# Attention of a fused chain in pairs of tiles: outputs of two tiles in one block, scores of the next two in another

## The chip, the cores and the metric

One Trainium2 chip, one NeuronCore. The metric is device microseconds of one execution. Its engines are TensorE (PE, with its weight loads shown as PEld), VectorE (DVE), ScalarE (ACT), GpSimd (POOL) and SyncE (SP, which only issues DMAs here). Each runs its own instructions in the order of the program and waits on semaphores.

## The reference

Three layers after each other, in float32. The first is a linear attention with decay over (4 batches, 8 heads, 768 steps, head size 48):

```
for t in range(S):
    cur = einsum('bhd,bhe->bhde', u * k[t], v[t])
    y[t] = einsum('bhd,bhde->bhe', r[t], state + cur)
    state = w * state + einsum('bhd,bhe->bhde', k[t], v[t])
```

Its output, as 3072 tokens of 384, goes through an expert with three first matrices, `h = max(x @ w1, x @ w2, x @ w3)` (384 to 768) and `h @ w_out`, and then through a normalised gated one, `silu(xn @ w_gate) * (xn @ w_val) @ w_out` (384 to 1536 to 384).

## The kernel before

**Attention in tiles.** The 768 steps are cut into 6 chunks of 128; with 4 batches that makes 24 tiles, tile i being chunk i // 4 of batch i % 4. Within a tile the recurrence is done as matmuls:

- `prep` (L266): VectorE multiplies the raw r and k of the tile by powers of the decay (L264, the "raw product"); POOL makes r * u * k (L272, L273).
- `prep_b` (L276): VectorE reduces that over each head (L280), and POOL puts the sums on the diagonals of the eight 128 x 128 matrices Dg (L283). `prep2` (L288): POOL scales k for the products (L291).
- `pe_a` (L293): the **scores**, 8 matmuls of 48 x 128 by 128 columns, two beside each other in the two row halves of the array, into two PSUM banks. The profile shows each float32 matmul of attention as two records. `mix` (L303): VectorE copies the scores under the causal mask into Dg, two instructions, one per bank.
- `pe_y` (L336): the **outputs**, matmuls of 128 x 32 by 128 columns in four column strips, from Dg and v and, from tile 4 on, from the state. The longest strip has nine after each other. `fin` (L361): ScalarE writes the rounded output into x (L370), VectorE the rest (L371).
- `pe_st` (L315): the **products** of k and v, 8 matmuls of 128 x 64 by 48 columns. ScalarE masks them into kv (L313, two instructions; kv has one buffer), POOL decays the state (L332) and adds kv (L334). For tiles 0 to 3 the mask writes the state itself; the last four tiles have no products.

**The expert in slots.** The first expert goes in six rounds u, one for each chunk of 128 steps and 4 batches, 512 columns. A round has 18 slots of the first matrices (`a_l1`, L399) and 6 of the second (`a_out`, L426); each has nine 128 x 128 matmuls (three products of rounded and residual parts, L71 to L73) of 512 columns into one of four PSUM banks, which ScalarE copies (L417) or VectorE takes the maximum of (L420). In round 0 the first six and the next six slots have 256 columns, so that there are 30.

**What sets the order.** The order on each engine is that of the program. The list `steps` holds three steps per tile; six are done before round 0. After each slot a number of further steps is done: in round 0 one after each of slots 0 to 3 and the rest spread over slots 6 to 24; in rounds 1 to 4 twelve steps over the first 20 of 24 slots, after slots 0, 1, 3, 5, 6, 8, 10, 11, 13, 15, 16 and 18. So round u does the tiles of round u + 1. `block(i)` is scores and mix of tile i + 1, then outputs, x and products of tile i, and puts the loads of tile i + 3 into the list `loads`, from which `load_next` takes. Raw inputs have three buffers, Dg two. Scores, outputs and products take turns in four PSUM banks (`psx`).

**The weights.** `tick` (L163) converts one piece of the weights from 64-bit words: a load on SP (L96) whose buffer comes free with the piece's sign step, three conversions on ScalarE (L107 to L109), two steps on VectorE (L118, L122), and for the first expert a cast on ScalarE (L129) and a residual on POOL or VectorE (L130). Round 0 has a tick after nearly every slot, rounds 1 to 4 nine each, of which three end with sums of weights on VectorE (L137). After attention come the last round and the second expert, which the change does not touch.

The state of the pair's two tiles belongs to different batches, so neither tile waits for the other's state.

Of the kernel before, what the change touches and what calls it, by code (L numbers as in the profile page):

```python
# [9 lines left out]
F32 = mybir.dt.float32  # L10
# [8 lines left out]
B, H, S, D = 4, 8, 768, 48  # L19
# [14 lines left out]
NB = S // 128  # L34
NT = B * NB
NP = H // 2
# [3 lines left out]
def r32(ap):  # L40
    return ap.bitcast(F32)
# [3 lines left out]
def rwkv_moe_kernel(ctx, tc, rkT, rkv, wd, ub, cst, rg, w1p, wo1p, w2p, out):  # L45
# [6 lines left out]
    psx = ctx.enter_context(tc.tile_pool(name="psx", bufs=4, space=PSUM))  # L52
# [138 lines left out]
    def load_next(n=1):  # L191
        for _ in range(n):
            if loads:
                loads.pop(0)()

    def load_tile(i):
        if i >= NT:
            return
        a = tp.tile([128, 2, NP, 128], F32, tag="raw", bufs=3, name=f"raw{i}")
        t = tp.tile([128, VO + NP * 144], F32, tag="tm", bufs=3, name=f"tm{i}")  # L200
        raw_t[i], tm_t[i] = a, t
        loads.append(lambda: sync.dma_start(a[0:64], rows64[96 * i:96 * i + 64]))
        if i < NT - 1:
            loads.append(lambda: sync.dma_start(a[64:128], rows64[96 * i + 48:96 * i + 112]))
        else:
            loads.append(lambda: (sync.dma_start(a[64:112], rows64[96 * i + 48:96 * i + 96]),
                                  sync.dma_start(a[112:128], rows64[96 * i:96 * i + 16])))
        loads.append(lambda: sync.dma_start(t[:, 0:VO], rkv[i, :, 0:VO]))
        loads.append(lambda: sync.dma_start(t[:, VO:], rkv[i, :, VO:]))
# [45 lines left out]
    st = {}  # L255

    def prep_raw(i):
        raw = raw_t.pop(i)
        st[i] = dict(raw=raw, tm=tm_t.pop(i))
        if i == 0:  # L260
            dve.tensor_tensor(out=raw[:, 1], in0=raw[:, 1], in1=qk[:, 1], op=ALU.mult)
            dve.tensor_tensor(out=raw[:, 0], in0=raw[:, 0], in1=qk[:, 0], op=ALU.mult)
        else:
            dve.tensor_tensor(out=raw, in0=raw, in1=qk, op=ALU.mult)  # L264

    def prep(i):  # L266
        prep_raw(i)
        s = st[i]
        tm = s["tm"]
        ru = tp.tile([128, DM], F32, tag="ru", name=f"ru{i}")  # L270
        eng = dve if i < NRU else pool
        eng.tensor_tensor(out=ru, in0=tm[:, 0:DM], in1=usb, op=ALU.mult)  # L272
        eng.tensor_tensor(out=ru, in0=ru, in1=tm[:, DM:2 * DM], op=ALU.mult)  # L273
        s["ru"] = ru

    def prep_b(i):  # L276
        s = st[i]
        a8 = tp.tile([128, H], F32, tag="a8", bufs=2, name=f"a8{i}")
        ru = s["ru"]
        dve.tensor_reduce(out=a8, in_=ru.rearrange("p (h d) -> p h d", d=D), op=ALU.add,  # L280
                          axis=mybir.AxisListType.X)
        Dg = tp.tile([128, H, 128], F32, tag="Dg", bufs=2, name=f"Dg{i}")
        pool.affine_select(out=Dg, in_=a8.unsqueeze(2).to_broadcast([128, H, 128]),  # L283
                           pattern=[[0, H], [1, 128]], channel_multiplier=-1, base=0,
                           compare_op=ALU.is_equal, fill=0.0)
        s["Dg"] = Dg

    def prep2(i):  # L288
        if i // B < NB - 1:
            k = st[i]["tm"][:, DM:2 * DM]  # L290
            pool.tensor_tensor(out=k, in0=k, in1=kt, op=ALU.mult)  # L291

    def pe_a(i):  # L293
        s = st[i]
        raw = s["raw"]
        pa = [psx.tile([128, NP, 128], F32, tag="x", name=f"pa{i}_{j}") for j in range(2)]
        for pr in range(NP):
            for j in range(2):
                sl = slice(64 * j, 64 * j + 48)
                pe.matmul(pa[j][:, pr], raw[sl, 1, pr], raw[sl, 0, pr], start=True, stop=True)  # L300
        s["pa"] = pa

    def mix(i):  # L303
        s = st[i]
        dg = s["Dg"].rearrange("p (r j) t -> p r j t", j=2)
        for j in range(2):
            dve.copy_predicated(out=dg[:, :, j], mask=cmask.unsqueeze(1).to_broadcast([128, NP, 128]),  # L307
                                data=s["pa"][j])

    def mask_kv(o, pk):  # L310
        for j in range(2):
            sl = slice(48 * j, 48 * j + 48)
            act.activation(o[:, :, sl], pk, AF.Copy, scale=m01[j])  # L313

    def pe_st(i):  # L315
        s = st[i]
        c, b = divmod(i, B)
        if c == NB - 1:
            return
        tm = s["tm"]  # L320
        v3 = tm[:, VO:].rearrange("p (r q e) -> p r q e", q=3, e=D)
        pk = psx.tile([128, NP, D], F32, tag="x", name=f"pkv{i}")
        for pr in range(NP):
            for j in range(2):
                o = DM + 96 * pr + 48 * j
                pe.matmul(pk[64 * j:64 * j + 64, pr], tm[:, o:o + 64], v3[:, pr, 2 * j], start=True, stop=True)
        if c == 0:
            mask_kv(Tst[b], pk)
        else:
            kv = tp.tile([128, NP, 96], F32, tag="kv", name=f"kv{i}")  # L330
            mask_kv(kv, pk)
            pool.tensor_tensor(out=Tst[b], in0=Tst[b],  # L332
                               in1=w128.unsqueeze(2).to_broadcast([128, NP, 96]), op=ALU.mult)
            pool.tensor_tensor(out=Tst[b], in0=Tst[b], in1=kv, op=ALU.add)  # L334

    def pe_y(i):  # L336
        s = st[i]
        c, b = divmod(i, B)
        tm = s["tm"]
        py = s["py"] = psx.tile([128, 3, 128], F32, tag="x", name=f"py{i}")  # L340
        lanes = []
        for n in range(4):
            lane = []
            for k in range(3):
                pr, o = (k, 32 * n) if n < 3 else (3, 32 * k)
                ops = [(tm[:, VO + 144 * pr + 48 * j + o:VO + 144 * pr + 48 * j + o + 32],
                        s["Dg"][:, 2 * pr + j]) for j in range(2) if o != (64, 0)[j]]
                if c > 0:
                    ops.append((Tst[b][:, pr, o:o + 32], s["raw"][:, 0, pr]))
                for m, (l, r) in enumerate(ops):  # L350
                    lane.append((py[32 * n:32 * n + 32, k], l, r, m == 0, m == len(ops) - 1))
            lanes.append(lane)
        for m in range(max(map(len, lanes))):
            for lane in lanes:
                if m < len(lane):
                    o, l, r, start, stop = lane[m]
                    pe.matmul(o, l, r, start=start, stop=stop)  # L357
# [3 lines left out]
    def fin(i):  # L361
        s = st[i]
        u, m = divmod(i, B)
        if m == 0:
            xt[u] = ap_.tile([128, 2, 3, 512], F32R, tag="x", bufs=2, name=f"x{u}")
        xh, xl = xt[u][:, 0], xt[u][:, 1]
        o = 128 * m
        cs = slice(o, o + 128)
        y = s["py"]
        act.copy(xh[:, :, cs], y)  # L370
        dve.tensor_tensor(out=xl[:, :, cs], in0=y, in1=r32(xh[:, :, cs]), op=ALU.subtract)  # L371

    def att_steps():
        def block(i):
            if i + 1 < NT:
                pe_a(i + 1)
                mix(i + 1)
            pe_y(i)
            fin(i)
            pe_st(i)  # L380
            load_tile(i + 3)

        def ahead(i):
            load_next(2)
            prep(i)

        def ahead_b(i):
            load_next(1)
            prep_b(i)
            prep2(i)  # L390

        for i in range(NT):
            yield lambda i=i: block(i)
            yield lambda i=i: ahead(i + 2) if i + 2 < NT else None
            yield lambda i=i: ahead_b(i + 2) if i + 2 < NT else None

    hs, sB = {}, {}

# [44 lines left out]
    with tc.manual_schedule():  # L443
# [14 lines left out]
        for _ in range(WARM):  # L458
            pe.matmul(pw[:, 0:128], r32(ones), r32(ones), start=True, stop=True)
        steps = list(att_steps())  # L460
        pos = 0
        tick(TKI[0])
# [578 lines left out]
```

## Time and profile before

| | |
|---|---|
| median of 3 runs | 868.15 us (867.7 to 873.35) |
| the profiled execution | 869.46 us |
| its span, first to last instruction | 867.4 us |
| mean granted TensorE clock | 0.973 of 2.4 GHz |
| instructions | 13472 |

The span is that of the profiled execution alone; the 2.06 us beside it lie before the first and after the last instruction. In the rows below, times are us from the span's start, mean durations ns; a name such as `pl<-x,w_a` says which tile an instruction writes and from which it reads (pl a slot's bank, pa scores, py outputs, pkv products).

### The profile page before, as it was taken

The page shows a single profiled execution, that of the slowest core. Times are in us where ns is not written, and L with a number is a line of the kernel's source. Part 1 is how long each engine was busy: PE and PEld are TensorE (multiplying, and loading weights), DVE is VectorE, ACT ScalarE, POOL GpSimd, SP SyncE. Part 2 cuts the span into 40 slices and gives each one's busy share as a digit, 9 for nine tenths or more (in the row PEclk, how much of TensorE's full clock was granted, in tenths as well). Part 3 has the DMA queues.
Part 4 walks back from the last instruction along what each step waited for, and adds up shares of the span by engine and source line. Part 5 has one row for each costly group of instructions (what it writes and reads, how often), then busy time and mean ns, then how long its engine had stood idle before and what let it go on. Part 6 is the DMA issues. An engine that isn't in the chain of part 4 may idle for free.

```text
span 867.4 us, 13472 instructions
## 1 busy us (share of the span) xinstructions
PE 835.2 (96%) x5206; PEld 688.8 (79%) x5206; DVE 496.6 (57%) x752; ACT 406.3 (47%) x762; POOL 253.5 (29%) x215
## 2 busy tenths in 40 slices
PE   7779899999999999999989999999999999999996
PEld 6667788888888888887778788888788888888885
DVE  5779957857858757525745464644445372333342
ACT  1776643434434433315367564555544454444441
POOL 3589645435435432005547442000100000000000
PEclk7689999999999999999989999999999999999998
DMA  9675646666665665153376551345251062433001
GB/s 260 211 229 161 197 142 176 183 186 173 187 186 173 185 187 151 58 181 132 113 281 235 194 208 56 118 174 187 105 189 56 0 255 91 142 131 110 1 36 40
DMA packets 48915, 131.87 MB, mean 152 GB/s; under 512 B 6982, under 2 KB 19782, under 8 KB 44236
## 3 DMA queue, kind: packets, MB, share of 16 engines
q1 hardware_dynamic: 46684, 115.01, 41.6%
q0 software_dynamic: 1728, 14.16, 4.1%
q10 hardware_dynamic: 432, 1.77, 0.6%
q8 instruction: 43, 0.70, 0.3%
q14 instruction: 28, 0.23, 0.1%
HBM read 97.08 MB, written 33.84 MB: 151 GB/s over the span
## 4 chain that ended last, share of the span: by engine, by line
PE 85%; DVE 6%; ACT 2%; DMA 2%; POOL 2%; issue 2%; SPq 0%; DVEq 0%; ACTq 0%; POOLq 0%
PE pl L71 7%; PE pl L73 7%; PE pl L72 7%; PE py L357 5%; PE po L71 5%; PE po L73 5%; PE po L72 5%; PE px L72 4%; PE px L71 4%; PE px L73 4%; PE pb L71 3%; PE pb L73 3%; PE pa L71 3%; PE pa L73 3%; PE pb L72 3%; PE pa L72 3%
## 5 line engine op out<-in xcount | busy, mean ns | idle before, releaser
L71 PE MATMUL pl<-x,w_a 128*128 128x512 f32 (+1 forms) x342 | 133.4, 390 | 5.9 <-ACT w_a L129 2.8
L73 PE MATMUL pl<-x,w_a 128*128 128x512 f32 (+1 forms) x342 | 130.7, 382 | 0.7 <-POOL w_a L130 0.7
L72 PE MATMUL pl<-x,w_a 128*128 128x512 f32 (+1 forms) x342 | 130.5, 382 | 0.2 <-DVE x L371 0.2
L815 DVE TENSOR_TENSOR v<-pb,es 128x512 f32<-128x512 f32 x36 | 24.9, 692 | 165.7 <-PE pb L73 165.7
L71 PEld LDWEIGHTS pl<-x,w_a 128*128 128x128 f32 x342 | 65.2, 191 | 19.7 <-ACT w_a L129 3.0
L420 DVE TENSOR_TENSOR c<-pl,c 128x512 f32<-128x512 f32 (+1 forms) x76 | 50.0, 658 | 49.2 <-PE pl L73 43.7
L73 PEld LDWEIGHTS pl<-x,w_a 128*128 128x128 f32 x342 | 65.4, 191 | 13.5 <-POOL w_a L130 1.1
L72 PEld LDWEIGHTS pl<-x,w_a 128*128 128x128 f32 x342 | 65.4, 191 | 11.7 <-DVE x L371 0.4
L724 ACT CAST hb<-si 128x512 fp32r<-128x512 f32 x36 | 22.3, 620 | 80.6 <-DVE si L818 80.6
L122 DVE TENSOR_TENSOR wf<-wraw 128x384 f32<-128x384 f32 x60 | 59.9, 999 | 0.0
L422 ACT CAST h1h<-c 128x512 fp32r<-128x512 f32 (+1 forms) x32 | 19.0, 593 | 75.3 <-DVE c L420 75.0
L541 POOL TENSOR_TENSOR sq<-sq 128x512 f32<-128x512 f32 x12 | 16.3, 1361 | 123.9 <-ACT sq L539 79.5
L283 POOL TENSOR_SCALAR_AFFINE_SELECT Dg<-a 128x1024 f32<-128x1024 f32 x24 | 31.1, 1295 | 72.2 <-DVE a L280 58.3
L357 PE MATMUL py<-Dg,tm 128*32 128x128 f32 x768 | 51.1, 304 | 0.0
L118 DVE SCALAR_TENSOR_TENSOR wraw<-wf,wraw 128x384 uint32<-128x384 uint32 x60 | 50.1, 836 | 0.1
L504 POOL TENSOR_TENSOR ws<-gv,ws 128x576 fp32r<-128x576 f32 x24 | 36.9, 1537 | 42.3 <-ACT ws L503 37.0
L307 DVE COPY_PREDICATED Dg<-csb,pa 128x512 f32<-128x512 uint32 x48 | 32.7, 735 | 27.1 <-PE pa L300 23.9
L357 PEld LDWEIGHTS py<-Dg,tm 128*32 128x32 f32 x768 | 42.6, 121 | 4.6 <-issue 1.4
L71 PE MATMUL pb<-f,ws 128*128 128x512 f32 x108 | 42.6, 395 | 0.3 <-ACT pb L793 0.3
L72 PE MATMUL pa<-f,ws 128*128 128x512 f32 x108 | 42.5, 394 | 0.0
L71 PE MATMUL pa<-f,ws 128*128 128x512 f32 x108 | 42.5, 394 | 0.0
L73 PE MATMUL pa<-f,ws 128*128 128x512 f32 x108 | 42.5, 394 | 0.0
(176 smaller groups left out, 2131.3 us busy)
## 6 DMA issues: line engine op xcount, KB each, us to landing
ws<-w2s SPq DMA_DIRECT2D x24, 1152.0 KB, 5.1
wraw<-in_w2p SPq DMA_DIRECT2D x36, 384.0 KB, 3.5
w2s<-ws POOLq DMA_DIRECT2D x12, 1152.0 KB, 6.0
raw<-in_rkT SPq DMA_DIRECT2D x47, 256.0 KB, 4.2
tm<-in_rkv SPq DMA_DIRECT2D x24, 384.0 KB, 4.9
tm<-in_rkv SPq DMA_DIRECT2D x24, 288.0 KB, 4.9
wraw<-in_w1p SPq DMA_DIRECT2D x18, 384.0 KB, 4.0
w2d<-wf SPq DMA_DIRECT2D x36, 192.0 KB, 3.7
```

Of the source, the lines that this page charges most:

```text
L71: pe.matmul(o, lh, rh, start=start, stop=False, **kw)
L72: pe.matmul(o, lh, rl, start=False, stop=False, **kw)
L73: pe.matmul(o, ll, rh, start=False, stop=stop, **kw)
L118: dve.scalar_tensor_tensor(out=clow(n), in0=cw[n].bitcast(U32), scalar=3, in1=clow(n), op0=ALU.logical_shift_left, op1=ALU.bitwise_or)
L122: dve.tensor_tensor(out=cw[n], in0=clow(n).bitcast(F32), in1=csgn(n), op=ALU.mult)
L283: pool.affine_select(out=Dg, in_=a8.unsqueeze(2).to_broadcast([128, H, 128]), pattern=[[0, H], [1, 128]], channel_multiplier=-1, base=0, c ...
L307: dve.copy_predicated(out=dg[:, :, j], mask=cmask.unsqueeze(1).to_broadcast([128, NP, 128]), data=s["pa"][j])
L357: pe.matmul(o, l, r, start=start, stop=stop)
L420: dve.tensor_tensor(out=c1[:, :n], in0=p[:, :n], in1=c1[:, :n], op=ALU.max)
L504: lo_eng.tensor_tensor(out=t[:, 1, sl], in0=r[:, sl], in1=r32(t[:, 0, sl]), op=ALU.subtract)
L724: act.copy(hh, x)
L815: dve.tensor_tensor(out=v1, in0=Bk, in1=es, op=ALU.add)
```

## The change

Tiles 0 to 3 keep their order, without the scores of tile 4 in the block of tile 3. From tile 4 on the steps go in pairs. One step does the outputs of tiles i and i + 1, their x, then the products of both into one PSUM bank, the state updates and the list entries of the loads of tiles i + 3 and i + 4. Four steps prepare the tiles i + 2 and i + 3. A sixth does the scores of both, into all four banks of `psx`, and both mixes. The number of steps stays 72, so the spreading over slots is the same: in round 0 scores(4,5) come after slot 7 and outputs(4,5) after slot 8, scores(6,7) after slot 16 and outputs(6,7) after slot 17; in rounds 1 to 4 outputs come after slots 0 and 10, scores after slots 8 and 18. No arithmetic is changed.

```diff
-    def pe_st(i):
+    def pe_st(i, pk=None):
...
-        pk = psx.tile([128, NP, D], F32, tag="x", name=f"pkv{i}")
+        if pk is None:
+            pk = psx.tile([128, NP, D], F32, tag="x", name=f"pkv{i}")
...
+        s["pk"] = pk
+
+    def state(i):
+        c, b = divmod(i, B)
+        if c == NB - 1:
+            return
+        pk = st[i]["pk"]
...
-        def block(i):
-            if i + 1 < NT:
-                pe_a(i + 1)
-                mix(i + 1)
-            pe_y(i)
-            fin(i)
-            pe_st(i)
-            load_tile(i + 3)
+        def scores(*tiles):
+            for i in tiles:
+                pe_a(i)
+            for i in tiles:
+                mix(i)
+
+        def outputs(*tiles):
+            for i in tiles:
+                pe_y(i)
+            for i in tiles:
+                fin(i)
+            pk = None
+            if len(tiles) > 1 and tiles[0] // B < NB - 1:
+                pk = psx.tile([128, 2, NP, D], F32, tag="x", name=f"pkv{tiles[0]}")
+            for n, i in enumerate(tiles):
+                pe_st(i, pk if pk is None else pk[:, n])
+            for i in tiles:
+                state(i)
+                load_tile(i + 3)
...
-        for i in range(NT):
-            yield lambda i=i: block(i)
-            yield lambda i=i: ahead(i + 2) if i + 2 < NT else None
-            yield lambda i=i: ahead_b(i + 2) if i + 2 < NT else None
+        for i in range(3):
+            yield lambda i=i: (scores(i + 1), outputs(i))
+            yield lambda i=i: ahead(i + 2)
+            yield lambda i=i: ahead_b(i + 2)
+        yield lambda: outputs(3)
+        yield lambda: ahead(5)
+        yield lambda: (ahead_b(5), scores(4, 5))
+        for i in range(4, NT, 2):
+            yield lambda i=i: (outputs(i, i + 1), load_next(2))
+            for j in (i + 2, i + 3):
+                yield lambda j=j: ahead(j)
+                yield lambda j=j: ahead_b(j)
+            yield lambda i=i: scores(i + 2, i + 3) if i + 2 < NT else None
```

## Rows read from the trace of the kernel before

**Rows 1.** The page, busy us (share of the span) and instructions of each engine.

```profile
PE 835.2 (96%) x5206; PEld 688.8 (79%) x5206; DVE 496.6 (57%) x752; ACT 406.3 (47%) x762; POOL 253.5 (29%) x215
```

**Rows 2.** Windows: stretch, its length, busy us (count) by engine, clock, DMA share, GB/s.

```profile
64.00:89.40 25.40, 20.91 (x188) 17.16 (x187) 23.97 (x29) 16.75 (x37) 22.85 (x20) 1.00 0.61 178
...
125.70:361.80 236.10, 236.10 (x2060) 195.38 (x2059) 167.46 (x250) 97.29 (x191) 93.18 (x76) 1.00 0.58 168
...
59.80:63.20 3.40, 3.40 (x55) 3.03 (x55) 1.53 (x2) 2.59 (x6) 3.32 (x4) 0.50 0.97 275
```

**Rows 3.** TensorE's waits, 31.8 to 107 us: total us, times, longest.

```profile
PE pa L300 <- issue: 5.2, 2, 3.3
```

**Rows 4.** Timeline of TensorE around tile 17's block: start, length, records; windows cut some.

```profile
270.05 0.39 PE L73 MATMUL pl<-x,w_a 128*128 128x512 f32 x1
...
270.37 1.05 PE L300 MATMUL pa<-raw 48*128 48x128 f32 x14
...
270.37 1.16 PE L300 MATMUL pa<-raw 48*128 48x128 f32 x16
...
273.24 0.38 PE L357 MATMUL py<-raw,T 128*32 128x128 f32 x2
...
273.55 0.56 PE L326 MATMUL pkv<-tm 128*64 128x48 f32 x12
...
273.55 0.67 PE L326 MATMUL pkv<-tm 128*64 128x48 f32 x16
...
274.49 0.39 PE L72 MATMUL pl<-x,w_a 128*128 128x512 f32 x1
```

**Rows 5.** The same around tile 22's block (no products) and tile 23's (outputs alone).

```profile
348.14 0.39 PE L73 MATMUL pl<-x,w_a 128*128 128x512 f32 x1
...
351.98 0.40 PE L72 MATMUL pl<-x,w_a 128*128 128x512 f32 x1
...
361.79 0.39 PE L73 MATMUL pl<-x,w_a 128*128 128x512 f32 x1
...
364.53 0.39 PE L72 MATMUL pl<-x,w_a 128*128 128x512 f32 x1
```

**Rows 6.** Timeline of VectorE in round 0; in brackets its idle time before.

```profile
63.67 0.55 DVE L280 TENSOR_REDUCE a<-ru 128x8 f32<-128x384 f32 x1 [2.34 <-POOL ru L273]
...
71.92 1.53 DVE L264 TENSOR_TENSOR raw<-raw,qk 128x1024 f32<-128x1024 f32 x1
...
94.78 1.38 DVE L307 COPY_PREDICATED Dg<-csb,pa 128x512 f32<-128x512 uint32 x2
```

**Rows 7.** Timeline of POOL in round 0.

```profile
64.55 1.42 POOL L283 TENSOR_SCALAR_AFFINE_SELECT Dg<-a 128x1024 f32<-128x1024 f32 x1
...
69.10 1.22 POOL L334 TENSOR_TENSOR T<-T,kv 128x384 f32<-128x384 f32 x1
```

**Rows 8.** Timeline of ScalarE in round 0.

```profile
67.50 0.42 ACT L313 ACTIVATE kv<-pkv,csb 128x192 f32<-128x192 f32 x1
...
71.18 0.37 ACT L417 COPY c<-pl 128x256 f32<-128x256 f32 x1
71.45 0.56 ACT L107 ACTIVATE wf<-wraw 128x384 f32<-128x384 f32 x1
```

**Rows 9.** Timeline of TensorE in round 0: two scores blocks, slots 9 and 18.

```profile
59.35 1.91 PE L300 MATMUL pa<-raw 48*128 48x128 f32 x16 [1.96 <-issue]
...
64.83 0.39 PE L71 MATMUL pl<-x,w_a 128*128 128x256 f32 x1
...
89.40 1.30 PE L300 MATMUL pa<-raw 48*128 48x128 f32 x16 [3.29 <-issue]
...
94.89 0.50 PE L71 MATMUL pl<-x,w_a 128*128 128x512 f32 x1
```

**Rows 10.** Timeline of VectorE in rounds 1 and 2.

```profile
187.16 0.29 DVE L137 TENSOR_TENSOR wf<-wf,wf 128x128 f32<-128x128 f32 x1 [2.43 <-DMA w2d<-wf]
...
215.97 1.48 DVE L420 TENSOR_TENSOR c<-pl,c 128x512 f32<-128x512 f32 x2
```

More of the change, by code (lines that the diff above doesn't have):

```diff
@@ L373, in att_steps @@
     def att_steps():
-        def block(i):
-            if i + 1 < NT:
-                pe_a(i + 1)
-                mix(i + 1)
-            pe_y(i)
-            fin(i)
-            pe_st(i)
-            load_tile(i + 3)
+        def scores(*tiles):
[16 more added lines that the diff above has]
+                load_tile(i + 3)
         def ahead(i):
-            load_next(2)
-            prep(i)
+            if i < NT:
+                load_next(2)
+                prep(i)
         def ahead_b(i):
-            load_next(1)
-            prep_b(i)
-            prep2(i)
-        for i in range(NT):
-            yield lambda i=i: block(i)
-            yield lambda i=i: ahead(i + 2) if i + 2 < NT else None
-            yield lambda i=i: ahead_b(i + 2) if i + 2 < NT else None
+            if i < NT:
+                load_next(1)
+                prep_b(i)
+                prep2(i)
+        for i in range(3):
[11 more added lines that the diff above has]
+            yield lambda i=i: scores(i + 2, i + 3) if i + 2 < NT else None
     hs, sB = {}, {}
```

## The prediction, made before the changed kernel was run

> **What bounds the kernel now.** I read the busy shares first: TensorE is busy 96% of the span, VectorE 57% [rows 1]. A share mixes stages, so the table of windows comes next [rows 2]. From 125.7 to 361.8 us, where attention is spread between the expert's slots, TensorE is busy 236.10 of 236.10 us at full clock: there every microsecond of TensorE work saved is saved from the end. From 64.0 to 89.4 us VectorE is busy 23.97 of 25.40 us, POOL 22.85, TensorE 20.91: that stage is paced by the weight conversion together with attention's VectorE and POOL steps. The table of waits says so too: between 31.8 and 107 us TensorE stands 5.2 us before two scores blocks [rows 3]. So the change must be costed twice: as TensorE work in rounds 1 to 4, as order on VectorE, ScalarE and POOL in round 0.
>
> **What the switches cost.** Slot matmuls start 0.227 us apart. Around one attention block the last slot matmul starts at 270.05 and the second one after it at 274.49 [rows 4]; less two pitches that is 3.99 us. Its contents: scores, 8 pairs at 0.11 (14 records span 1.05 us, 16 span 1.16), 0.88; outputs, 18 steps of the longest column strip (9 matmuls, two records each) at 0.11, the step by which two records outlast one of 0.27 [rows 4], 1.98; products, 8 pairs at 0.055 (12 records 0.56, 16 records 0.67), 0.44 [rows 4]. Together 3.30, so four changes of kind (slot, scores, outputs, products, slot) cost 0.69. The block without products is 351.98 - 348.14 - 0.45 = 3.39, of it 0.53 for three changes; the block of tile 23, outputs alone, is 364.53 - 361.79 - 0.45 = 2.29, of it 0.31 for two [rows 5].
>
> A pair of tiles has eight changes now, 1.38 us. Then it has five. The outputs block: 0.31 plus 0.16 for the products, 0.47. The scores block between two slots is not in the trace. It costs at least 0.22 (what scores add to an outputs block) and at most 0.53 (the three changes of the block without products); I take 0.42, nearest to the other two-change block, a little above it because the first scores pair starts late in its block too. The second tile of a block adds only contents. Saved per pair: 1.38 - 0.47 - 0.42 = 0.49 us.
>
> Rounds 1 to 4, tiles 8 to 23: before 12 x 0.69 + 3 x 0.53 + 0.31 = 10.2; after 6 x 0.47 + 2 x 0.31 + 7 x 0.42 = 6.4. **Gain 3.8 us** (2.9 to 5.2 by the two bounds). All of it lies on the path, TensorE being without a pause there. In round 0 the same count gives 5 x 0.69 - 0.47 - 2 x 0.47 - 3 x 0.42 = 0.8 us, but that stage has pauses to lose it in; it is inside the next sum.
>
> **Round 0, the order.** Now mix(4) runs five slots ahead of its outputs. Then scores(4,5) come after slot 7, in VectorE's order behind the reduce of tile 5, and outputs(4,5) after slot 8. The reduce waits for POOL and ends at 63.67 + 0.55 = 64.22 [rows 6]; nothing ahead of it changes but mix(4), and VectorE's wait for POOL hides that removal. A tile's mix takes 1.38 us for its two halves [rows 6], so mix(4) ends at about 65.6; mix(5) needs the diagonal that POOL ends at 64.55 + 1.42 = 65.97 [rows 7] and ends at 67.4. Scores(5) start at 59.35 now, behind their raw product [rows 9], and still do; with slot 8 behind them TensorE is through before 63. **The added wait**: it stands some 3 us until 65.6. Behind it: outputs 2 x 1.98, products 2 x 0.44, changes 0.4, slot 9 at about 71.0, against 64.83 [rows 9]. Of these 6.2 us, 2.4 are tile 5's own work done early.
>
> Who waits for that: SP's load of tile 7 (raw 4's buffer; needed 15 us later, free), POOL's decay of the state, and ScalarE. There the buffer kv is single: the masked products of tile 5 must wait until POOL has added those of tile 4 (1.22 us [rows 7]). Chain: products end 70.9, masks 2 x 0.42, add 1.22, masks 2 x 0.42, then what is queued on ScalarE: four conversions and casts of some 0.56, and the copy of slot 9's bank, 0.37 [rows 8], which ends at about 76.4 instead of 71.55. VectorE's maximum and the raw product of tile 6 stand behind that copy, so the product shifts from 71.92 [rows 6] to about 76.7: **VectorE is 4.8 us late**. It was nearly always busy from here to mix(7), which ended at 94.78 + 1.38 = 96.16 [rows 6]; part of its wait for the copy and the low half of tile 5, done early, come back, so I take 98.5 (96.2 if all is caught up, 101.0 if nothing). Outputs(6,7) wait for it after slot 17: outputs(6) from 97.1, outputs(7), products, slot 18 at about 102.2 against 94.89 [rows 9]. Less 2.4 us for tile 7's work done early, 4.9 us. A pause of this length lowers the clock: after the 1.96 us pause before 59.35 [rows 9] the granted clock was 0.50 from 59.8 to 63.2 [rows 2], 1.2 GHz for 3.4 us, worth up to 1.7 us. I add half of that beyond what the pause of 3.29 us before 89.40 [rows 9] brings already: **loss about 5.7 us**. Bounds: if VectorE catches up fully, the pause before 89.40 goes too and the stage gains 1.2; if nothing is caught up and two more stretches run at half clock, it loses 10.
>
> **Sum.** +5.7 - 3.8 = +1.9. The profiled execution took 869.46 us (span 867.4, 2.1 around it), 1.3 above the median of 868.15; it would become 871.4, and the median 870.0. All later phases keep their instructions.
>
> **The rivals.**
> *Absorbed (0.27).* Round 0 is paced by VectorE's and POOL's total, which does not change; the late scores wait where TensorE now waits anyway. For it: 4.5 of 25.4 us of TensorE idle in the window from 64.0 to 89.4 [rows 2]. Against it: the reduce at 63.67 is now directly ahead of the mix that outputs wait for. 868.15 - 1.2 - 3.8 = 863.
>
> *Slower (0.10): VectorE late in every round.* In rounds 1 to 4 scores come after slot 8 and their outputs after slot 10, 2 x 2.04 us later. From the end of slot 8 TensorE has the scores block, 2 x 0.88 + 0.42, and two slots before it asks for the first mix, 6.3 us; a mix takes 1.38, so the rival decides once VectorE is over 4.9 us behind at slot 8. For it: the weight sums of slot 6's conversion lie just ahead; in round 2 VectorE did two maxima in a row at 215.97 [rows 10], so it was about a slot, 2 us, behind, and another such sum waited 2.43 us for a DMA [rows 10], together 4.4. A wait of 1.5 us and half a stretch of low clock, 1.7, in four rounds: 870 + 12.8 = 883. Against it, all four rounds must come out so.
> The Trainium skill (TensorEngine Tiling (Array Packing), PSUM Bottleneck) says that tiling makes TensorE faster but not the emptying of PSUM, which can become the limit. The rows have the prices: TensorE fills the four banks in 1.76 us and VectorE empties them in 2 x 1.38 = 2.76; by that rule this rival holds wherever one or two slots lie between.
>
> *The change saves no switch (0.08).* If the second tile of a block started as late as a new kind does, rounds 1 to 4 would stay as they are and only round 0's loss count: 868.15 + 5.7 = 874. Against it: within a kind no step of rows 4 is late.
>
> **How the numbers follow.** The forecast has 0.55. Its own range is 864 to 876, from the bounds above. With the absorbed case the range is 863 to 877, which leaves out its lower half and nearly all of the slower rival, under 2 in 10. This kernel's measurement can tell about 1% from no change, 8.7 us: faster needs the absorbed case with the upper gain and more, 0.03; slower is most of the slower rival, 0.08; the same 0.89.
>
> **What would show it.** In the changed profile: blocks of the pair in rounds 1 to 4 with one change into and one out of each, TensorE still without pauses from 126 us, and attention's last block some 3.8 us earlier relative to slot 0 of round 1. In round 0: a pause before outputs(4) ended by VectorE's mix, ScalarE waiting for POOL's add between two masks, a longer pause before outputs(6). Wrong: no wait before either outputs block, or waits for the mix in rounds 1 to 4, or a scores block whose two changes cost over 0.53 us.

## The result, and the profile after

The changed kernel takes 877.58 us (median of 4 runs, 874.82 to 879.19) beside 868.35 us for the kernel before on the same chip: ratio 1.0096, 95% interval 1.0068 to 1.0123. It is **slower by 9.2 us**, about 1%. I had forecast +1.9 us, a median of 870.0 and a range up to 877.0, so the direction was right, the size was too small by 7 us, and the median lies 0.6 us above the range (by the ratio, 868.15 x 1.0096 = 876.5, just inside it). The profiled execution took 879.19 us, its span is 877.4 (before 867.4) and its mean granted clock 0.964 (before 0.973).

The page of the changed kernel first: busy us, share of the span and instructions of each engine.

```profile
PE 838.7 (96%) x5206; PEld 692.4 (79%) x5206; DVE 497.2 (57%) x752; ACT 407.2 (46%) x762; POOL 254.9 (29%) x215
```

Beside [rows 1] no engine has more instructions, and TensorE is 3.5 us busier with the same 5206. It should have been less busy, by the switches saved. Some of its work must have run slower, so I looked for the clock. These are the windows of the changed kernel (columns as in rows 2), the two pair blocks of outputs in round 0 first, then the stretch behind a wait in round 1, then one block in round 1 that had no wait, then most of rounds 1 to 4.

```profile
64.70:71.60 6.90, 6.86 (x112) 5.85 (x112) 3.71 (x7) 1.30 (x3) 3.48 (x4) 0.57 0.40 116
98.90:105.90 7.00, 7.00 (x113) 5.86 (x113) 3.80 (x7) 2.35 (x5) 2.09 (x3) 0.58 0.55 163
162.90:166.30 3.40, 3.40 (x10) 2.72 (x9) 3.29 (x8) 1.59 (x3) 0.00 (x0) 0.51 0.02 7
137.00:141.00 4.00, 4.00 (x113) 3.86 (x112) 0.56 (x1) 1.07 (x2) 0.83 (x1) 1.00 0.18 48
170.00:374.20 204.20, 204.20 (x1792) 171.09 (x1785) 143.55 (x215) 85.32 (x167) 78.62 (x64) 1.00 0.58 169
```

The same 112 or 113 matmul records of a pair's outputs take 4.0 us at clock 1.00 in round 1 and 6.9 to 7.0 us at 0.57 and 0.58 in round 0: most of each block ran at 1.2 GHz. In 170.0 to 374.2 us TensorE has no gap and full clock, as before in 125.7 to 361.8 [rows 2].

What stood ahead of the slow stretches is in the changed kernel's table of TensorE's waits, first from 31.8 to 107 us (total, times, longest):

```profile
PE py L365 <- issue: 3.9, 1, 3.9
...
PE py L365 <- POOL w_a L130: 2.1, 1, 2.1
...
PE pa L300 <- ACT w_a L129: 1.5, 1, 1.5
```

and then the longest from 107 to 374.2 us:

```profile
PE psok L248 <- DVE Dg L307: 1.9, 1, 1.9
```

Of the two waits before scores of [rows 3] the longer is gone, and of the other 1.5 us are left (pa). In addition TensorE now waits before both outputs blocks (py), 2.1 and 3.9 us. The row of the 2.1 us names POOL; but the outputs read Dg, and VectorE's mix of tile 4 starts at 63.92 and takes 1.33 us for its two halves (below), so its first half ends just before the outputs start at 64.74. I had not foreseen the wait in the second table at all.

Where the time went, from the changed kernel's timeline of TensorE (start, length, records, in brackets the idle time before). The starts of slots 9 and 18 and of slot 0 of round 1 serve as marks.

```profile
64.74 0.43 PE L365 MATMUL py<-Dg,tm 128*32 128x128 f32 x2 [2.11 <-POOL w_a L130]
...
72.83 0.39 PE L71 MATMUL pl<-x,w_a 128*128 128x256 f32 x1
...
98.89 0.43 PE L365 MATMUL py<-Dg,tm 128*32 128x128 f32 x2 [3.94 <-issue]
...
106.97 0.50 PE L71 MATMUL pl<-x,w_a 128*128 128x512 f32 x1
...
134.89 0.39 PE L71 MATMUL pl<-x,w_a 128*128 128x512 f32 x1
...
162.69 0.19 PE L248 MATMUL psok<-ok,csb 128*1 128x4 f32 x2 [1.94 <-DVE Dg L307]
```

Slot 0 of round 1 in the kernel before:

```profile
123.59 0.39 PE L71 MATMUL pl<-x,w_a 128*128 128x512 f32 x1
```

Against [rows 9], slot 9 is 72.83 - 64.83 = 8.0 us later and slot 18 is 106.97 - 94.89 = 12.1; less the 2.4 us for the tile done early that is 9.7 of loss where I had 4.9 and 0.8 for the clock, 5.7. Slot 0 of round 1 is 134.89 - 123.59 = 11.3 later, 0.88 of it the scores of tile 9, done already: **round 0 loses 10.4**. The wait of psok (the decay flag) is 1.94, and 3.40 us at half clock behind it lose 1.7; the distance between the same slots of the two kernels grows there by 3.4. Rounds 1 to 4 give back 3.6 by their blocks (worked out below). 10.4 + 3.4 - 3.6 = 10.2, beside a difference of the spans of 10.0.

How the lateness came about on the other engines, VectorE first (changed kernel, round 0):

```profile
63.45 0.55 DVE L280 TENSOR_REDUCE a<-ru 128x8 f32<-128x384 f32 x1 [2.34 <-POOL ru L273]
63.92 1.33 DVE L307 COPY_PREDICATED Dg<-csb,pa 128x512 f32<-128x512 uint32 x2
...
77.89 0.43 DVE L450 TENSOR_TENSOR c<-pl,c 128x256 f32<-128x256 f32 x1 [4.02 <-ACT c L447]
78.23 1.53 DVE L264 TENSOR_TENSOR raw<-raw,qk 128x1024 f32<-128x1024 f32 x1
...
98.06 2.57 DVE L307 COPY_PREDICATED Dg<-csb,pa 128x512 f32<-128x512 uint32 x4
```

and ScalarE:

```profile
71.87 0.48 ACT L378 CAST x<-py 128x384 fp32r<-128x384 f32 x1 [2.40 <-PE py L365]
...
73.27 0.41 ACT L313 ACTIVATE kv<-pkv,m 128x192 f32<-128x192 f32 x1
...
74.87 0.42 ACT L313 ACTIVATE kv<-pkv,csb 128x192 f32<-128x192 f32 x1 [1.19 <-POOL T L342]
...
77.50 0.36 ACT L447 COPY c<-pl 128x256 f32<-128x256 f32 x1
```

This is the predicted chain, link for link: reduce, mix, outputs, ScalarE's cast, its 1.19 us for POOL's add between two masks because kv has one buffer, its copy of slot 9's bank, then VectorE's maximum (which stood 4.02 us for that copy) and the raw product of tile 6 behind it. But the product starts at 78.23 where I had 76.7, and mix(7) ends at 100.6 where I had 98.5. The excess starts in the outputs block: 2.9 us of slow clock there.

### The profile page after: what moved, and what is told of

The parts are those of the page before. It is cut to its first block, busy times and chain, and to the rows that moved or that the text cites. A ratio compares the mean times of both kernels' runs of the same rounds, so it can differ in the third digit from the quotient of the medians.

```text
span 877.4 us, 13442 instructions
## 1 busy us (share of the span) xinstructions
PE 838.7 (96%) x5206; PEld 692.4 (79%) x5206; DVE 497.2 (57%) x752; ACT 407.2 (46%) x762; POOL 254.9 (29%) x215
## 4 chain that ended last, share of the span: by engine, by line
PE 79%; DVE 7%; POOL 6%; ACT 3%; DMA 2%; issue 2%; SPq 0%; DVEq 0%; POOLq 0%; ACTq 0%
PE pl L71 6%; PE py L365 6%; PE pl L72 6%; PE pl L73 6%; PE po L73 5%; PE po L71 5%; PE po L72 5%; PE px L72 4%; PE px L71 4%; PE px L73 4%; PE pb L71 3%; PE pb L73 3%; PE pa L71 3%; PE pa L73 3%; PE pb L72 3%; PE pa L72 3%
## 5 line engine op out<-in xcount | busy, mean ns | idle before, releaser
L71 PE MATMUL pl<-x,w_a 128*128 128x512 f32 (+1 forms) x342 | 134.6, 394 | 6.7 <-ACT w_a L129 2.8
L73 PE MATMUL pl<-x,w_a 128*128 128x512 f32 (+1 forms) x342 | 132.4, 387 | 2.9 <-POOL w_a L130 2.9
L72 PE MATMUL pl<-x,w_a 128*128 128x512 f32 (+1 forms) x342 | 132.3, 387 | 0.0
L71 PEld LDWEIGHTS pl<-x,w_a 128*128 128x128 f32 x342 | 66.3, 194 | 21.1 <-ACT w_a L129 3.0
L73 PEld LDWEIGHTS pl<-x,w_a 128*128 128x128 f32 x342 | 66.6, 195 | 16.3 <-POOL w_a L130 3.8
L72 PEld LDWEIGHTS pl<-x,w_a 128*128 128x128 f32 x342 | 66.5, 195 | 11.9 <-DVE x L379 0.3
L365 PE MATMUL py<-Dg,tm 128*32 128x128 f32 x768 | 53.1, 309 | 6.0 <-issue 3.9
L118 DVE SCALAR_TENSOR_TENSOR wraw<-wf,wraw 128x384 uint32<-128x384 uint32 x60 | 44.4, 739 | 0.1
L71 PE MATMUL pb<-f,ws 128*128 128x512 f32 x108 | 42.6, 394 | 0.1
L73 PE MATMUL pb<-f,ws 128*128 128x512 f32 x108 | 42.3, 392 | 0.0
```

The costliest lines, as they stand in the source:

```text
L71: pe.matmul(o, lh, rh, start=start, stop=False, **kw)
L72: pe.matmul(o, lh, rl, start=False, stop=False, **kw)
L73: pe.matmul(o, ll, rh, start=False, stop=stop, **kw)
L118: dve.scalar_tensor_tensor(out=clow(n), in0=cw[n].bitcast(U32), scalar=3, in1=clow(n), op0=ALU.logical_shift_left, op1=ALU.bitwise_or)
```

## The experiments

**Theory** after this reading: of some 9 us, 6 to 7 are half clock behind the pauses of round 0 with what VectorE loses by it, 3 are the flag's wait in round 1 with the half clock behind it, and the rest is the late mix less the switches saved, as predicted. **Rivals**: the late chain through VectorE costs as much by itself and the clock only goes with it; the single buffer kv makes VectorE late; pairing costs something in rounds 1 to 4 too. Each ratio below is against the kernel before on the same chip, with its 95% interval. Fillers are extra matmuls whose results are not used; nothing is left out of the computation in any of the ten kernels.

**The flag a slot earlier.** The two small flag matmuls (L248) take one of the four psx banks. After slot 8 of round 1 the scores of tiles 10 and 11 hold all four until VectorE has mixed. Here they come after slot 7, ahead of the scores.

```
-            if u == 1 and n == 8:
+            if u == 1 and n == 7:
                 flag = decay_flag()
```

> The changed kernel with the decay flag's two small matmuls one slot earlier in round 1 (after slot 7, ahead of scores(10,11)). Theory bank: the flag takes a fifth of the four banks right behind a scores block that holds all four, so TensorE stands 2.2 us for VectorE's mix and then runs 3.4 us at half clock. It expects both gone and some 3.4 us less than the changed kernel, about 874. Rival (the wait only moves to the next block that needs a bank): no change, 877.6.

874.72 us, ratio 1.0070 [1.0048, 1.0091], 2.9 us under the changed kernel. The two intervals overlap, so I read the price in the trace. The window of this kernel where the half clock had been:

```profile
162.70:166.10 3.40, 3.40 (x16) 2.83 (x16) 3.40 (x7) 2.47 (x5) 0.00 (x0) 1.00 0.13 41
```

Its timeline of TensorE just ahead, where the wait had been:

```profile
161.57 1.16 PE L300 MATMUL pa<-raw 48*128 48x128 f32 x14 [0.85 <-DVE nok L250]
```

The 1.94 us wait is gone, the clock is 1.00 where it was 0.51, and 16 matmuls fit where there were 10. What is left is 0.85 us inside the scores block, which now waits for VectorE to free the flag's bank. So the wait and the clock behind it were the price. From slot 0 of round 1 to slot 0 of round 2 it is 65.82 us here, 67.88 in the changed kernel, and 64.50 in the two kernels below that have the flag after slot 2: a price of 3.4 us, of which this edit gives back 2.1. In two profiles below that keep the late flag but have no half clock behind it (two buffers for kv, scores(4) earlier) it is 66.3, so the wait alone is 1.8 of the 3.4 and the clock 1.6.

**Pairs from tile 8 on.** Round 0 keeps single blocks; the flag is after slot 7 here too.

```
-        for i in range(3):
+        for i in range(7):
...
-        yield lambda: outputs(3)
-        yield lambda: ahead(5)
-        yield lambda: (ahead_b(5), scores(4, 5))
-        for i in range(4, NT, 2):
+        yield lambda: outputs(7)
+        yield lambda: ahead(9)
+        yield lambda: (ahead_b(9), scores(8, 9))
+        for i in range(8, NT, 2):
```

> Pairs from tile 8 on instead of tile 4 on, so that round 0 keeps the order of the kernel before, and the flag early as in e1. Theory: rounds 1 to 4 gain 0.45 us a pair, round 0 loses nothing: 868.35 - 3.5 = 864.9, faster than both. Rival (pairs also cost something in rounds 1 to 4, or in the round 0 to 1 handover): 868 or more.

867.4 us, ratio 0.9991 [0.9977, 1.0005], 2.5 us above the 864.9 expected. The loss of round 0 is gone: it lay in the pairs of tiles 4 to 7. The gain of rounds 1 to 4 shows only in part, since two waits stand in its way, in this kernel's table of TensorE's waits from 107 us on:

```profile
PE pa L300 <- issue: 1.1, 1, 1.1
PE pa L300 <- DVE nok L250: 0.9, 1, 0.9
```

The first is in the first pair of scores at 113.61, too close behind tile 7's block, the second is the flag's. Without these 2.0 us it would stand at 865.4; that is an estimate, which the best version below puts to the test.

**Two buffers for kv.**

```
-    kv = tp.tile([128, NP, 96], F32, tag="kv", name=...)
+    kv = tp.tile([128, NP, 96], F32, tag="kv", bufs=2, name=...)
```

> The changed kernel with two buffers for kv. Theory VectorE late through ScalarE, as predicted: ScalarE's 1.2 us wait for POOL between the masks of the two tiles goes, the copy of slot 9 and all behind it come 1.2 us earlier, the pause before outputs(6) shrinks from 4.3 to about 3.1 us, and the time falls by 1 to 2 us, to about 876. Rival (the order, not the buffer, makes VectorE late): no change, 877.6.

873.25 us, ratio 1.0052 [1.0033, 1.0071]. ScalarE's timeline in this kernel:

```profile
73.48 0.42 ACT L313 ACTIVATE kv<-pkv,csb 128x192 f32<-128x192 f32 x1
...
76.13 0.36 ACT L447 COPY c<-pl 128x256 f32<-128x256 f32 x1
```

The start of TensorE's second outputs block:

```profile
97.83 0.43 PE L365 MATMUL py<-Dg,tm 128*32 128x128 f32 x2 [5.29 <-issue]
```

The masks have no wait between them and the copy is 1.4 us earlier, as expected. Outputs(6) start 1.06 us earlier, but the pause before them did not shrink: it grew to 5.29 us. So kv was a link of the chain, worth about 1 us there. The time fell by more, 4.3 us where 1 to 2 were expected; slot 18 came 2.3 earlier because that outputs block ran partly at full clock, and the profile shows no half clock behind the flag's wait. I don't know why the clock differed there. The changed kernel's own runs spread over 4 us with the clock too (below), so the 4.3 us are not shown to be the buffer's.

**A filler in the outputs' own bank, a miss.** Matmuls ahead of outputs(4) and outputs(6), to keep TensorE busy through the pause.

```
+            for _ in range({4: 12, 6: 22}.get(i, 0)):
+                pe.matmul(py.rearrange("p k n -> p (k n)"), ones,
+                          wts["a", 0][:, 0, 0:384], start=True, stop=True)
```

> The changed kernel with filler matmuls (12 before outputs(4), 22 before outputs(6), 384 columns each, about 2 and 3.7 us at full clock) into the bank that the outputs then overwrite; they fill the pauses, add nothing to what is computed. Theory clock: the loss in round 0 is mostly that both outputs blocks run at half clock after their pause (6.8 us instead of 3.85); with fillers they run at full clock, 3 us less for each, about 872. Rival late mix: TensorE waits for VectorE anyhow, fillers change nothing or cost up to 1 us: 877 to 879.

880.84 us, ratio 1.0146 [1.0126, 1.0166]. The outputs' banks are psx banks too, and the scores held them until the mix; so the filler waited with the outputs and then ran ahead of them, the first twelve at half clock throughout (timeline of this kernel):

```profile
65.77 4.21 PE L350 MATMUL py<-w_a,ones 128*128 128x384 f32 x12 [2.21 <-DVE Dg L307]
```

It tells nothing of the theory, except that 12 matmuls that start behind a pause take 0.35 us each, where the same take 0.19 in the next experiment.

**A filler in another bank.** The same in one of the slots' four banks, which is free at that time.

```
+            if tiles[0] in (4, 6) and len(tiles) > 1:
+                pf = psm.tile([128, 512], F32, tag="m", ...)
+                for _ in range({4: 12, 6: 23}[tiles[0]]):
+                    pe.matmul(pf[:, 0:384], ones, wts["a", 0][:, 0, 0:384],
+                              start=True, stop=True)
             for i in tiles:
                 pe_y(i)
```

> As e4_filler, but the filler matmuls (12 and 23 of 384 columns, ahead of the outputs of the pairs 4,5 and 6,7) go into a slot's bank, which is free, so that they run while VectorE mixes. Theory clock: both outputs blocks of round 0 run at full clock (about 3.9 us instead of 6.8) and the time falls by 3 to 6 us against the changed kernel, to 872 to 875. Rival (the pauses alone cost it, the clock follows something else): 877 to 879.

870.99 us, ratio 1.0029 [1.0013, 1.0045], clear of the changed kernel's interval: 6.6 us faster by the medians, 5.8 by the two ratios, by doing more matmuls. Its windows of the two outputs blocks:

```profile
65.50:69.60 4.10, 4.10 (x115) 3.87 (x114) 2.99 (x7) 1.20 (x3) 2.13 (x4) 1.00 0.13 28
96.70:101.20 4.50, 4.27 (x114) 3.84 (x114) 3.44 (x7) 2.33 (x5) 1.48 (x3) 1.00 0.39 103
```

Its timeline of TensorE, fillers (pf) and outputs:

```profile
63.32 2.28 PE L392 MATMUL pf<-w_a,ones 128*128 128x384 f32 x12
65.53 0.46 PE L365 MATMUL py<-Dg,tm 128*32 128x128 f32 x8
...
70.66 0.39 PE L71 MATMUL pl<-x,w_a 128*128 128x256 f32 x1
...
96.77 0.38 PE L365 MATMUL py<-Dg,tm 128*32 128x128 f32 x3 [1.25 <-issue]
...
102.25 0.50 PE L71 MATMUL pl<-x,w_a 128*128 128x512 f32 x1
```

Its timeline of VectorE, the raw product of tile 6 and the mixes of 6 and 7:

```profile
76.06 1.53 DVE L264 TENSOR_TENSOR raw<-raw,qk 128x1024 f32<-128x1024 f32 x1
...
95.94 2.60 DVE L307 COPY_PREDICATED Dg<-csb,pa 128x512 f32<-128x512 uint32 x4
```

Outputs(4) start 0.8 us later than in the changed kernel, right behind the fillers, and both blocks end earlier. Slot 9 comes at 70.66, slot 18 at 102.25, the mix ends at 98.54. My prediction had 71.0, 102.2 and 98.5: with the clock held, its chain comes out to within 0.4 us (and again, counted from slot 0 of round 0, in the run with both remedies below: 0.7 and 0.3). VectorE's product is 2.2 us earlier than in the changed kernel, so part of its lateness there was the clock's doing. From slot 0 of round 0 (31.85 us here, 31.62 in the changed kernel) to slot 0 of round 1 (130.20, 134.89) it is 98.35 us, against 103.27: 4.9 us is what the fillers save in round 0, and 2.2 us more of the difference between these two profiles lie behind attention (last section). The rival that the late chain alone costs as much falls.

**Scores(4) earlier.** The chain's other end: tile 4 is mixed one step earlier, so outputs(4) have less to wait for.

```
-        yield lambda: outputs(3)
+        yield lambda: (scores(4), outputs(3))
         yield lambda: ahead(5)
-        yield lambda: (ahead_b(5), scores(4, 5))
+        yield lambda: (ahead_b(5), scores(5))
```

> The changed kernel with scores(4) and mix(4) back in the block of tile 3; scores(5) stay where the pair has them. Theory late mix: outputs(4) no longer wait 2.2 us for the mix, mix(5) is ready 2 us into the block, so slot 9 comes 2 us earlier, and one stretch at half clock less: 873 to 876. Rival (VectorE's lag behind ScalarE sets slot 18 anyhow): slot 9 earlier, slot 18 not, 877.

871.44 us, ratio 1.0040 [1.0022, 1.0058], better than the expected 873 to 876. In its table of TensorE's waits in round 0 there is no pause before outputs(4); tile 5's scores (pa) wait 3.2 us instead:

```profile
PE py L365 <- issue: 5.3, 1, 5.3
PE pa L300 <- issue: 3.2, 1, 3.2
```

Its slots 9 and 18:

```profile
68.97 0.38 PE L71 MATMUL pl<-x,w_a 128*128 128x256 f32 x1
...
102.52 0.50 PE L71 MATMUL pl<-x,w_a 128*128 128x512 f32 x1
```

Both slots, 9 and 18, are earlier than in the changed kernel, by 3.9 and 4.5 us, although the pause before outputs(6) is longer, 5.3 us. The rival that slot 18 comes late anyhow falls: what the first outputs block loses is handed on. No half clock follows the flag's wait in this profile, which is worth some 1.6 us here and is not shown to be this edit's doing.

**Outputs a few slots later in round 0.**

```
+            if u == 0:
+                want = min(want, 6 if n < 11 else 12 if n < 19 else want)
```

> The changed kernel with its outputs blocks of round 0 later: outputs(4,5) after slot 11 instead of 8, outputs(6,7) after slot 19 instead of 17; scores stay, later steps are caught up at once. Theory distance: the loss of round 0 is the pause of TensorE where outputs follow their scores too closely, and the half clock after it. It expects no pause before either outputs block, both at full clock, and 5 to 8 us less than the changed kernel: 870 to 873 (the flag's 3 us and the gain of 3.5 remain). Rival late VectorE: the pauses move to the slots behind (banks not emptied): 875 or more.

873.21 us, ratio 1.0054 [1.0036, 1.0071], just above the expected 870 to 873. No pause stands before either outputs block any more, and slot 13 stands instead (timeline of TensorE):

```profile
84.54 0.80 PE L71 MATMUL pl<-x,w_a 128*128 128x512 f32 x1 [6.24 <-ACT c L447]
```

What ScalarE's copy waited for begins on VectorE (its timeline):

```profile
81.08 0.55 DVE L280 TENSOR_REDUCE a<-ru 128x8 f32<-128x384 f32 x1 [4.84 <-POOL ru L273]
```

VectorE waits for POOL, which does the state decays and adds of the pair from 74.33 to 79.02 and only then the r * u * k that the reduce reads; ScalarE and the slot's bank wait in turn. Distance by itself moves the pause. At that place VectorE and POOL set the pace.

**Pairs from tile 8 on, with slots between, the best version.** The second experiment with its two waits taken away: the flag after slot 2, and one step held back to the end of round 0, so that tile 7's block and the first pair's scores stand apart.

```
-            if u == 1 and n == 8:
+            if u == 1 and n == 2:
...
+            if u == 0 and n < 27:
+                want = min(want, len(todo) - 1)
```

> e2_pairs_from_8 with its two new waits removed: the flag after slot 2 of round 1 (e2 still stood 1.1 us for its bank) and the last step of round 0 with scores(8,9) after slot 27 instead of 24 (e2 stood 1.2 us for the raw product of tile 9). Theory: those 2.3 us are what kept e2 from the 3.5 us of saved changes; 864.7 to 865.5, faster than before by 0.3 to 0.4%. Rival: waits elsewhere, or nothing saved, 867.5.

863.75 us, ratio 0.9950 [0.9927, 0.9972]: faster than both kernels, by 4.8 us beside the kernel before (2.4 to 6.3 by the interval) and by 1 us more than expected. Window of this kernel:

```profile
105.00:359.00 254.00, 254.00 (x2210) 212.22 (x2209) 179.65 (x265) 106.91 (x210) 105.74 (x86) 1.00 0.58 169
```

TensorE has no gap and full clock in 254 us. From slot 0 of round 1 to slot 0 of round 5, behind the last of attention, it is 252.50 us against 257.06 in the kernel before, 4.56 less; 0.88 of that are the scores of tile 9, done ahead. So 3.7 us are the gain of rounds 1 to 4 (3.8 predicted) by itself. What makes up the rest of the 4.8 is not shown.

**Both remedies in the changed kernel**: the filler in another bank, and the flag after slot 2.

> The changed kernel with the fillers of e5_filler_other_bank and the flag after slot 2 of round 1. If half clock in round 0 and the flag's bank are the two terms that the prediction left out, what remains is its own sum with the late mix alone: round 0 loses some 4 to 5 us, rounds 1 to 4 save 3.5: 868 to 870, the same as before. Rival (another term is missing): 872 or more.

868.6 us beside 867.31, ratio 1.0020 [1.0005, 1.0035]. **The changed kernel once more**, on the same chip:

> The changed kernel again, on the chip and in the rounds of e9, so that the differences are of one chip: 875 to 879, ratio about 1.01, with outputs blocks of round 0 at half clock (6 to 7 us) and the flag's 2.2 us wait.

876.92 us, ratio 1.0102 [1.0074, 1.0129], 8.3 us above the one with both remedies. Among its six runs two had a mean clock of 0.979 and 0.975 and took 872.46 and 874.54 us; the four at 0.965 to 0.969 took 876.64 to 879.09. The profile shows what was expected, a clock of 0.50 from 60.0 to 69.9 and from 97.3 to 104.0 us and the flag's wait of 1.94. From slot 0 of round 0 to slot 0 of round 1 it takes 101.90 us, the one with both remedies 98.00: 3.9 us for the fillers on this chip.

## Why the prediction came out as it did

**The step that failed** is "I add half of that beyond what the pause of 3.29 us before 89.40 brings already: loss about 5.7 us". The clock's term was 0.8 us, put too low by a factor of five to eight: taking the slow clock away with fillers saves 6.6 us by the medians (5.8 by the ratios), and in round 0 itself 4.9 and 3.9 by the marks of two pairs of profiles. I took the 1.7 us of one stretch of half clock from [rows 2] and halved it for a risk. But both new pauses stand directly before the densest work of attention, a pair's outputs, and each block lost 2.9 us there; and since ScalarE's casts and copy, VectorE's product and the next mix hang on the first block's end, the first block's loss was not made up: outputs(6) started 2.1 us later than with the fillers. The lower clock was in my bounds ("two more stretches run at half clock, it loses 10": round 0 lost 10.4) and not in my sum. (The lower bound of the gain in rounds 1 to 4, given as 2.9, comes out at 3.0.) The Trainium skill (TensorE: Matmul & The Clock Gate, HAM oscillation — how this bites in real kernels) says that a burst of matmuls behind a long enough idle gap starts throttled, and that one should arrange the work so that the array stays warm; in round 0 the trace agrees, 0.57 behind the pause and 1.00 with the filler. Not every pause does it: see the last section.

**The step that was missing** is the flag. The prediction followed the orders of four engines and the buffer kv, but not the pool of four PSUM banks, and so put this term at nothing. A paired scores block holds all of it until the mix, and the flag's two matmuls of 0.19 us behind it wait: 1.94 us, and the half clock behind it (0.51 for 3.4 us), together 3.4.

**The late mix in round 0: right.** The pauses before outputs(4) and (6), ScalarE's wait for POOL's add (1.19 beside 1.22 predicted) and VectorE's lateness are all there, and with the clock held the marks fit. With the late mix at 4.9 and the switches at 3.8 the prediction has +1.1 left when clock and flag are taken out; the run with both remedies has +1.3 (interval 0.4 to 3.0). The interval is 2.6 us wide, so tenths prove nothing here. By the marks round 0 loses 5.3 us in that run and 5.7 in the one with the fillers alone, where I had 4.9 without the clock.

**The switches: right.** From the changed kernel, a scores block and an outputs block of rounds 2 and 3, with the slot matmuls around them:

```profile
254.22 0.39 PE L73 MATMUL po<-h1h,w_o 128*128 128x512 f32 x1
...
256.86 0.39 PE L72 MATMUL po<-h1l,w_o 128*128 128x512 f32 x1
...
268.67 0.39 PE L73 MATMUL pl<-x,w_a 128*128 128x512 f32 x1
...
274.45 0.39 PE L72 MATMUL pl<-x,w_a 128*128 128x512 f32 x1
```

Counted as in the prediction from [rows 4]: 256.86 - 254.22 - 0.45 = 2.19, less contents of 1.76, leaves 0.43 for the scores block's two changes (predicted 0.42). 274.45 - 268.67 - 0.45 = 5.33, less 4.84, leaves 0.49 for the outputs block's three (0.47). A pair saves 1.38 - 0.43 - 0.49 = 0.46 us (0.49), and rounds 1 to 4 go from 10.2 to 6 x 0.49 + 2 x 0.31 + 7 x 0.43 = 6.6, some 3.6 (3.8).

The same can be read without counting contents, from slot 0 of round 5, in the kernel before:

```profile
380.65 0.39 PE L71 MATMUL pl<-x,w_a 128*128 128x512 f32 x1
```

and in the changed kernel:

```profile
390.77 0.39 PE L71 MATMUL pl<-x,w_a 128*128 128x512 f32 x1
```

From slot 0 of round 1 it is 257.06 us before and 255.88 after, 1.2 less; with the flag's 3.4 added and the 0.88 for tile 9's scores taken off, the blocks give back 3.7.

**The rivals.** *Absorbed* fell: both outputs blocks waited. *VectorE late in every round* fell: no outputs block waits in rounds 1 to 4, so the rule of the Trainium skill (TensorEngine Tiling (Array Packing), PSUM Bottleneck) that emptying PSUM can become the limit held in round 0, where VectorE was busy 23.97 of 25.40 us already before [rows 2], and in round 1 for the flag alone, which asked for a bank with no slot in between. *Saves no switch* fell, by the 0.43 and 0.49. The slower side did come, by two mechanisms of which I had priced one too low and the other not at all.

**What stays open.** Flag and clock cost 2.9 and 6.6 us taken away one at a time, 9.5, but 8.3 taken away together on another chip; the runs of these kernels spread by 4 to 7 us. By the marks they are 3.4 in round 1 and 4.9 in round 0, together 8.3, so an overlap is not needed to explain it; but each mark comes from one profile, and the fillers' saving is 3.9 in the other pair. Nor do the traces show why the mean clock differs from execution to execution of one program, though they show one place where it does (last section).

## What to carry to other kernels

Price a new pause of TensorE not by its length alone but by the dense work that stands directly behind it, at half clock, and by who waits for that work's end; here this was five to eight times what I had put down. When work is grouped, count the buffers and banks that the group holds and look for every other user of the same pool, however small. Group only where the engine that empties the group has slack, with slots on either side: in rounds 1 to 4 alone this change gains what it was worth, and tiles 4 to 7 and the flag turned that into a loss.

## What the hardware showed that I had not expected

A block of matmuls with practically no gap in it (TensorE busy 6.86 of 6.90 us) stayed at half clock nearly to its end behind a pause of 2.1 us; I had put down half of one stretch of 3.4 us for both. Twelve and 23 matmuls in a bank that was free kept the clock at 1.00 through both blocks, and this useless work made the kernel 6.6 us faster.

A pause of one length was not followed by one clock. Where the second expert begins, in code that no version here touches, TensorE waits 2.61 to 2.64 us for VectorE in all twelve profiles. In the kernel before the next matmul starts at 436.14, and its window from there is

```profile
436.10:442.00 5.90, 5.86 (x14) 4.60 (x15) 1.19 (x2) 3.62 (x5) 1.41 (x1) 0.50 0.97 327
```

while with the flag a slot earlier it starts at 444.49:

```profile
444.40:450.40 6.00, 5.62 (x23) 4.35 (x24) 2.13 (x5) 4.71 (x7) 1.60 (x2) 1.00 1.00 337
```

The slow stretch there is 6.8 us long in the kernel before and in the changed one, 3.4 in the run with fillers alone and absent in the one with the flag a slot earlier. From slot 0 of round 5 to the end of the span these four cases take 486.8 (before), 486.6 (changed), 484.5 and 483.2 us, so up to 3.5 us between two profiles are not the change's doing.
